# Wide scores and split value products for the last tile, three residuals by an identity product, and a new order table

## The chip, the cores and the metric

The kernel runs on one core of a Trainium2 chip. The metric is the device time of one execution in microseconds, median of the runs. The core's engines are TensorE (PE, with its weight loads PEld), VectorE (DVE), ScalarE (ACT), GpSimd (POOL) and SyncE (SP, which here only issues DMAs); each runs its own instruction stream in order, and semaphores tie them together.

## What is computed

Four attention layers over x of 2048 tokens by 512 features, each with a layer norm ahead and a residual behind. Layers 1 and 3 (A) are linear attention, layers 2 and 4 (B) are causal attention in a window of 256 keys; both have 32 heads of 16 features. The two A layers share weights, and so do the two B layers.

```python
def _A_ref(x, wqkv, wo):                       # linear attention, H = 32, Dh = 16
    q, k, v = ...                              # (x @ wqkv), split in heads
    phi = lambda t: jnp.where(t > 0, t + 1, jnp.exp(t)) + 1e-6
    pq, pk = phi(q), phi(k)
    kv = jnp.einsum("bhsd,bhse->bhde", pk, v)
    z = jnp.einsum("bhsd->bhd", pk)
    num = jnp.einsum("bhqd,bhde->bhqe", pq, kv)
    den = jnp.einsum("bhqd,bhd->bhq", pq, z)[..., None] + 1e-6
    o = num / den
    return o.transpose(...).reshape(B, S, D) @ wo

def _B_ref(x, wqkv, wo):                       # window W = 256
    q, k, v = ...
    scores = jnp.einsum("bhqd,bhkd->bhqk", q, k) * (Dh ** -0.5)
    mask = (idx[:, None] - idx[None, :] >= 0) & (idx[:, None] - idx[None, :] < W)
    p = _softmax(jnp.where(mask[None, None], scores, -1e9), axis=-1)
    o = jnp.einsum("bhqk,bhkd->bhqd", p, v)
    return o.transpose(...).reshape(B, S, D) @ wo

x = x + _A_ref(_layernorm(x), A_wqkv, A_wo)
x = x + _B_ref(_layernorm(x), B_wqkv, B_wo)
x = x + _A_ref(_layernorm(x), A_wqkv, A_wo)
x = x + _B_ref(_layernorm(x), B_wqkv, B_wo)
```

## The kernel before

The tokens are cut into 16 tiles of 128. Python code builds a list of some 2,500 operations (`Plan`), each with the engines that it may run on, what it reads and writes, and the PSUM tiles that it holds; one operation emits between one and 64 instructions. The order of the whole list, the engine of each operation that has a choice (ACT or DVE for PSUM evictions, DVE or POOL for some masks) and the PSUM bank of each tile stand in a packed literal, `TABLE`. `place` (L92) unpacks it; `synchronise` (L133) then works out which semaphores each operation has to wait for, and `play` (L1072) writes every engine's stream in the table's order. So an engine's order is that of the table, and a wait of one operation holds back all that stand behind it on its engine. The table was written by a search of its own, and only its result stands in the kernel.

PSUM has eight banks of 128 x 512 f32; nearly all work passes through them, with TensorE writing and ACT or DVE reading.

The stages, by time in the profile: layer 1's keys, queries and sums over all tiles (to about 44 us), layer 1's closing sums (`barrier`, L530), then layer 2 tile by tile, together with layer 3's keys and values of tiles that are done (`middle(2)`, L884); layer 3's closing sums (about 242 us); layer 4 tile by tile (`middle(3)`), and the output.

The steps that the change and the prediction touch:

- `setup` (L288): 12 loads on SP. x comes in pieces (tiles 0, 1, 2-3, 4-5, 6-7, 8-11, 12-15), the A weights as keys (`wAk`), queries (`wAq`), values (`wAv`) and output (`wAo`), the B weights as `wBn` (1 MB), `wBv` and `wBo`. An eighth and later load waits for the landing of the one four places ahead of it in this list.
- `norm` (L366): statistics on DVE (L374, L375), epsilon added to the variance (L377 on DVE for tile 0 alone, L379 on POOL for all others), the power -1/2 on POOL (L380), normalisation on DVE (L381), then a transpose, by DMA from SP or, for the first and last tiles of a stage, by TensorE with an eviction (L395, L402).
- `tok` (L410): a product of one tile with 512 columns, four matmuls in two halves; `resid` (L602) adds its PSUM result to the tile of x on DVE (L604).
- `b_scores` (L659): scores of a tile's 64 keys (b = 0 or 1, one half of the tile's 128 keys, each key twice for an even and an odd head) against up to 256 queries, for two of the four head groups f at once: 8 matmuls into four banks, two exps on ACT (L686), one causal mask on DVE (L694). A tile has four such groups.
- `b_first` (L702): for tile 0, half b = 0, the same over all four f, 128 queries at a time: 16 matmuls, two exps of 1024 columns (L721), a mask over 16 head groups (L726).
- `b_far`, `b_edge`, `far_masks`: scores and masks at the far edge of the window (L754, L772, L773, L801).
- `b_values` (L807): value products of a tile, one PSUM tile for each half h of the head groups; for each f and each of four heads pairs, up to six matmuls of 34 columns, one per block of 64 keys (L822), 24 instructions for one f; then reciprocal and division (L834, L835).
- `b_out` (L840): transpose, output product, residual. `b_last` (L849): the same for tile 15 of layer 4, in halves, with two residuals of 256 columns (L877) and two stores of 64 KB (L878). The other 15 tiles are stored by `outp` (L942) from SP or POOL.
- at the end SP waits for every DMA's semaphore in turn (L1103 to L1106).

## Time and profile before

| | |
|---|---|
| time, median of 3 runs (lowest, highest) | 412.12 us (411.43, 413.20) |
| the profiled execution | 412.60 us |
| its span, first to last instruction | 410.8 us |
| instructions | 17,540 |
| granted TensorE clock, mean | 1.000 |
| bytes moved by DMA | 37.19 MB |

The page gives for each engine the time in which it was busy and the share of the span. The chain that ended last is followed back from the last instruction, at each step to what released it; its shares say what set the end, by engine. A stage table gives the busy time of each engine within a stretch of the span, as "busy (x instructions)" in the order PE, PEld, DVE, ACT, POOL, then the granted clock, the DMA share and GB/s. A timeline row is start, length, engine, line, operation, output and input, shapes, count, and in brackets the idle time before it with what ended it. In a row of a group, the figures after the bar are busy time in us and the mean of one instruction in ns. A row of DMA issues ends with KB each and the median time from issue to landing.

### The profile page before, as it was taken

Reading aid. Unit: us, or ns where it says so; the run is one execution under the profiler, and the core shown is the slowest. Engines: PE = TensorE matmul, PEld = TensorE weight load, DVE = VectorE, ACT = ScalarE, POOL = GpSimd, SP = SyncE. Lnnn points to the kernel's source line nnn. Section 1 sums busy time; section 2 is a strip of 40 time slices with the busy share of each in tenths; the row PEclk is TensorE's granted clock in tenths of the full one; section 3 lists DMA queues with packets and bytes.
Section 4 is the critical chain, followed back from the end, with each engine's and each line's share of the span. In section 5 each row is a group of like instructions: output and inputs, shape, how many; then the busy total and the mean of one; then the engine's idle time right before and its main releaser. Section 6 shows DMA issues by size and latency. Waiting matters only on the chain.

```text
span 410.8 us, 17540 instructions
## 1 busy us (share of the span) xinstructions
PE 386.9 (94%) x7668; PEld 260.3 (63%) x7742; DVE 344.5 (84%) x807; ACT 352.8 (86%) x448; POOL 122.4 (30%) x216
## 2 busy tenths in 40 slices
PE   7999999999999999999999999999999988999896
PEld 3654676766575576566567777586757755566674
DVE  6997799989998899888887789997899688857585
ACT  4654659998999999999998357999999999999993
POOL 4576653111252331320503203303113304303020
PEclk9999999999999999999999999999999999999999
DMA  7495114443243435353222100344314821561751
GB/s 249 101 217 144 49 34 115 120 70 90 56 106 74 119 77 107 81 119 82 68 41 57 27 2 2 105 109 81 102 44 122 122 66 41 120 127 56 168 107 42
DMA packets 66596, 37.19 MB, mean 91 GB/s; under 512 B 47640, under 2 KB 61848, under 8 KB 66520
## 3 DMA queue, kind: packets, MB, share of 16 engines
q1 hardware_dynamic: 66032, 34.75, 37.0%
q8 instruction: 61, 1.00, 1.1%
q0 software_dynamic: 480, 1.31, 1.0%
q14 instruction: 15, 0.12, 0.1%
q10 hardware_dynamic: 8, 0.00, 0.0%
HBM read 6.29 MB, written 2.10 MB: 20 GB/s over the span
## 4 chain that ended last, share of the span: by engine, by line
PE 51%; ACT 34%; DVE 9%; DMA 3%; issue 2%; SPq 1%; POOL 1%
ACT pb L686 20%; PE ps L420 18%; PE ps L434 10%; PE ps L822 10%; PE ps L676 5%; ACT pb L801 5%; ACT vp L686 4%; PE ps L501 3%; ACT tE L444 2%; DMA wA<-in_A_wqkv_dram 2%; DMA xT<-xn 1%; DVE xres L604 1%; DVE stats L374 1%; ACT pb L721 1%; PE ps L477 1%
## 5 line engine op out<-in xcount | busy, mean ns | idle before, releaser
L686 ACT ACTIVATE pb<-ps 128x1024 bf16<-128x1024 f32 (+2 forms) x216 | 198.9, 1020 | 5.2 <-PE ps L676 3.9
L822 PEld LDWEIGHTS ps<-vB,pb 128*128 128x128 bf16 x2560 | 77.7, 96 | 12.3 <-DVE pb L694 3.6
L822 PE MATMUL ps<-vB,pb 128*128 128x34 bf16 x2560 | 83.5, 177 | 0.6 <-POOL pb L772 0.3
L434 PE MATMUL ps<-xT,wBp 128*128 128x128 bf16 x1024 | 69.0, 219 | 1.7 <-ACT tE L444 0.6
L434 PEld LDWEIGHTS ps<-xT,wBp 128*128 128x128 bf16 x1024 | 58.5, 98 | 13.7 <-issue 4.4
L379 POOL TENSOR_SCALAR ve<-mv 128x1 f32<-128x1 f32 x63 | 16.7, 265 | 154.7 <-DVE mv L375 152.7
L444 ACT ACTIVATE tE<-ps 128x512 bf16<-128x512 f32 x64 | 38.6, 612 | 27.1 <-PE ps L420 11.2
L772 POOL TENSOR_SCALAR_AFFINE_SELECT pb<-pb 128x1024 bf16<-128x1024 bf16 x30 | 34.4, 1146 | 71.4 <-DVE pb L694 23.8
L676 PE MATMUL ps<-XQ,kB 32*128 32x256 bf16 (+3 forms) x992 | 48.0, 267 | 3.3 <-ACT pb L754 0.7
L604 DVE TENSOR_TENSOR xres<-ps,xres 128x512 bf16<-128x512 f32 x63 | 43.0, 684 | 6.7 <-PE ps L420 6.3
L420 PE MATMUL ps<-wA,XQ 128*128 128x512 bf16 x174 | 45.6, 379 | 2.2 <-issue 0.6
L374 DVE BATCH_NORM_STATS2 stats<-xres 128x6 f32<-128x512 bf16 x64 | 43.5, 685 | 2.8 <-DMA xres<-in_A_x_dram 2.2
L694 DVE TENSOR_TENSOR pb<-pb,tri 128x512 bf16<-128x512 bf16 (+1 forms) x108 | 41.5, 396 | 3.3 <-ACT pb L686 3.1
L801 ACT ACTIVATE pb<-ps 128x1024 bf16<-128x1024 f32 x42 | 41.4, 1059 | 1.1 <-PE ps L792 0.9
L380 POOL TENSOR_TENSOR rs<-ve,negh 128x1 f32<-128x1 f32 x64 | 37.8, 591 | 8.3 <-DVE ve L377 3.0
L434 PE MATMUL ps<-XQ,wA 128*128 128x128 bf16 x512 | 35.4, 219 | 0.3 <-DMA wA<-in_A_wqkv_dram 0.3
L434 PEld LDWEIGHTS ps<-XQ,wA 128*128 128x128 bf16 x512 | 30.7, 98 | 7.3 <-DMA wA<-in_A_wqkv_dram 0.8
L420 PE MATMUL ps<-wBv,xT 128*128 128x512 bf16 x110 | 31.4, 380 | 2.6 <-issue 1.0
L676 PEld LDWEIGHTS ps<-XQ,kB 32*128 32x128 bf16 x992 | 15.0, 92 | 29.5 <-ACT pb L686 7.5
L420 PE MATMUL ps<-M,XQ 128*128 128x512 bf16 x113 | 30.7, 380 | 2.3 <-ACT vp L686 0.4
L420 PE MATMUL ps<-wBo,oT 128*128 128x512 bf16 x105 | 28.8, 380 | 2.8 <-issue 1.0
L686 ACT ACTIVATE vp<-ps 128x1024 bf16<-128x1024 f32 (+2 forms) x32 | 26.7, 928 | 1.5 <-PE ps L676 1.5
(126 smaller groups left out, 551.6 us busy)
## 6 DMA issues: line engine op xcount, KB each, us to landing
vB<-vS SPq DMA_DIRECT2D x64, 136.0 KB, 2.7
kB<-vp SPq DMA_DIRECT2D x60, 128.0 KB, 2.3
wA<-in_A_wqkv_dram SPq DMA_DIRECT2D x3, 512.0 KB, 5.5
out_dram<-xres POOLq DMA_DIRECT2D x10, 128.0 KB, 2.8
xres<-in_A_x_dram SPq DMA_DIRECT2D x2, 512.0 KB, 5.1
pb<-in_B_wqkv_dram SPq DMA_DIRECT2D x1, 1024.0 KB, 5.8
xres<-in_A_x_dram SPq DMA_DIRECT2D x3, 256.0 KB, 5.5
out_dram<-xres SPq DMA_DIRECT2D x5, 128.0 KB, 2.7
```

Source lines behind the costliest of these rows:

```text
L374: self.on("DVE", "stats", lambda e: e.bn_stats(K.stats[:, t, :], x()), key, dve(512), rd=rd, wr=[("stats", t)], **held)
L380: self.pow = self.on("POOL", "pow", lambda e: e.tensor_tensor(K.rs[:, t, :], K.ve[:, t, :], K.negh[:], ALU.pow), key + 0.03, (640, 690), r ...
L420: m = e.matmul(K.ps(ps), lhs(c), rhs(c), start=c == 0 and not whole, stop=c == 3)
L434: m = e.matmul(K.ps(ps)[:, f * P:(f + 1) * P], w(c, f), xT(c), start=c == 0, stop=c == 3)
L444: self.on("ACT", "E", lambda e: e.activation(K.tE[:, s, :], K.ps(ps), ACT.Exp, bias=0.0), key, act(512), wr=[("tE", s)], ps=[ps])
L604: self.on("DVE", "res", lambda e: e.tensor_tensor(K.xres[:, t, :], K.ps(po), K.xres[:, t, :], ALU.add), key, dve(512), rd=[("xres", t)], w ...
L676: m = e.matmul(K.ps(ps[gq])[:, ns * i:ns * i + ns], K.kB[rows, j % 4, 2 * f + b, :, :], K.XQ[rows, f, q:q + ns], start=True, stop=True, ti ...
L686: return e.activation(out(2 * h, 2, ns), i, ACT.Exp, bias=0.0, scale=0.25)
L694: return e.tensor_tensor(x, x, K.tri[:, 0, sh:64].unsqueeze(1).unsqueeze(1).to_broadcast([P, 4, n, 64 - sh]), ALU.mult)
L772: return e.affine_select(out=x, in_=x, compare_op=ALU.is_ge, fill=0.0, base=-2, pattern=[[0, 16], [-2, 64]], channel_multiplier=1)
L801: return e.activation(far(h), i, ACT.Exp, bias=0.0, scale=0.25)
L822: m = e.matmul(K.ps(ps)[:, 34 * u:34 * u + 34], K.P((b // 2) % rp)[:, gq, f, o:o + P], K.vB[:, (b // 2) % 4, b % 2, r, :], start=i == 0, s ...
```

## The change

It has five parts.

1. Tile 15's scores, in both B layers, are made over all four head groups at once: `b_first` becomes `b_wide`, which takes the tile, the half b, the queries and their width. For each b one burst of 16 matmuls, two exps (1024 columns for b = 0, 512 for b = 1) and one mask, in place of two groups of 8 matmuls, two exps and one mask each.
2. Tile 15's value products of layer 4 are in two parts: `pu` for the four blocks of earlier tiles' keys (16 matmuls for one f), `pv` for the tile's own two blocks (8 matmuls). Both add into one PSUM tile; only the very first matmul of a bank clears it.
3. Three residuals of layer 4 are added by TensorE, as a product of the identity with the tile of x, behind the output product: tiles 13 and 14 whole, and the second half of tile 15. The result is then copied by ACT or DVE in place of the addition on DVE. The first half of tile 15 is still added on DVE.
4. Tile 15's output leaves in one store of 128 KB in place of two of 64 KB.
5. The epsilon addition may run on DVE or POOL for every tile, and the table is new: order, engines and banks.

```diff
-WHOLE = {2: (), 3: ()}
+WHOLE = {2: (), 3: (13, 14)}
+SPLIT = {3: (15,)}
...
-            self.on("POOL", "eps", lambda e: e.tensor_scalar(K.ve[:, t, :], K.mv[:, t, 1:2], LN_EPS, None, op0=ALU.add), key + 0.02, (300, 330), rd=[("mv", t)], wr=[("ve", t)])
+            self.g.add("eps", {"POOL": (300, 330), "DVE": (66, 150)}, lambda e, eng: e.tensor_scalar(K.ve[:, t, :], K.mv[:, t, 1:2], LN_EPS, None, op0=ALU.add), key + 0.02, rd=[("mv", t)], wr=[("ve", t)])
...
-        if whole:
-            self.pe("id", lambda e: e.matmul(K.ps(ps), K.ident[:], K.xres[:, t, :], start=True, stop=False), key - 0.01, 1, 512, rd=[("xres", t), ("ident",)], ps=[ps])
...
+                if whole and h:
+                    m = e.matmul(K.ps(ps), K.ident[:], K.xres[:, t, :], start=False, stop=True)
...
+    def resid(self, t, po, key, whole=False):
+        K = self
         if whole:
+            self.copy("rs", po, lambda: K.xres[:, t, :], lambda: K.ps(po), key, 512, wr=[("xres", t)])
+            return
...
-    def b_first(self, p, key):
+    def b_wide(self, j, b, q, w, n, key):
...
+        sl = j % self.rp
+        c = 384 * b + q - P * j - 64 * b
...
-                    m = e.matmul(K.ps(ps[gq])[:, P * f:P * f + P], K.kB[rows, 0, 2 * f, :, :], K.XQ[rows, f, P * p:P * p + P], start=True, stop=True, tile_position=(32 * gq, 0))
+                    m = e.matmul(K.ps(ps[gq])[:, w * f:w * f + w], K.kB[rows, j % 4, 2 * f + b, :, :], K.XQ[rows, f, q:q + w], start=True, stop=True, tile_position=(32 * gq, 0))
...
+        if split:
+            before = [x for x in blocks if x[1] > 0]
+            blocks = [x for x in blocks if x[1] <= 0]
+            for f in (2 * h, 2 * h + 1):
+                def put(e, f=f):
+                    m = None
+                    for gq in range(4):
+                        u = 4 * (f - 2 * h) + gq
+                        for i, (b, c) in enumerate(before):
+                            m = e.matmul(K.ps(ps)[:, 34 * u:34 * u + 34], at(b, c, gq, f), val(b, 4 * f + gq), start=i == 0 and u == 0, stop=False, skip_group_check=True)
+                    return m
+                self.pe("pu", put, key - 0.002 - 0.001 * (f % 2), 16, 34, rd=reads(f, before), ps=[ps])
...
+                    if not h:
+                        m = e.matmul(K.ps(po)[:, 256:512], K.ident[:], K.xres[:, j, 256:512], start=False, stop=False, skip_group_check=True)
...
-        for n in range(2):
-            cs = slice(256 * n, 256 * n + 256)
-            self.on("DVE", "res", lambda e, cs=cs: e.tensor_tensor(K.xres[:, j, cs], K.ps(po)[:, cs], K.xres[:, j, cs], ALU.add), key + 0.2 + 0.1 * n, dve(256), rd=[("xres", j)], wr=[("xres", j, n)], ps=[po])
-            self.on("SP", "out", lambda e, cs=cs: e.dma_start(K.out[0, j * P:(j + 1) * P, cs], K.xres[:, j, cs]), key + 0.3 + 0.1 * n, (520, 2400), rd=[("xres", j, n)])
+        self.on("DVE", "res", lambda e: e.tensor_tensor(K.xres[:, j, 0:256], K.ps(po)[:, 0:256], K.xres[:, j, 0:256], ALU.add), key + 0.2, dve(256), rd=[("xres", j)], wr=[("xres", j, 0)], ps=[po])
+        self.copy("rs", po, lambda: K.xres[:, j, 256:512], lambda: K.ps(po)[:, 256:512], key + 0.3, 256, rd=[("xres", j)], wr=[("xres", j, 1)])
+        self.on("SP", "out", lambda e: e.dma_start(K.out[0, j * P:(j + 1) * P, :], K.xres[:, j, :]), key + 0.4, (520, 2400), rd=[("xres", j, 0), ("xres", j, 1)])
...
-                    if j + b == 0 and ph in PART:
+                    if j + b == 0:
                         if f < 2:
-                            self.b_first(f, base + 0.25 * f)
+                            self.b_wide(j, b, P * f, P, f, base + 0.25 * f)
+                    elif j == T - 1:
+                        if f == 0:
+                            self.b_wide(j, b, P * j + 64 * b, P - 64 * b, 0, base + j + b / 4)
...
 TABLE = (
-    r"c-qZZ1GH_+j;*AUO4YS(+qP}nwr$(CZQHhO+h*^z&%Lkz@5lf8{~o>0SxP0TnVDHN_6n(#3ZYPu0>vt{(khG!tBeY#;;UdPxccG}D67J&gzBTqtRkpSE~5J8",
...
+    r"c-pmB1K4IqvhJ#`s_q`!wr$(CZQHhO+qP}nwwcT%GfC#2^Zk?EB%9q#_TGEG|KP7Ky!BRfJ?Df{N`+Nn6spjQ6)8~Rl~#$Bs3gj%2r8+Hs0OI#E|O}aUb~m>",
...
```

What the two tables say, unpacked by the rule of `place` and named by the operations of the code: 2,559 operations before, 2,546 after. Of the operations in both, about three quarters on PE and seven eighths on ACT stand in the same order as before, and somewhat more than half on DVE. These change their engine: 21 epsilon additions from POOL to DVE; 13 far masks from POOL to DVE and 13 the other way; 17 evictions from ACT to DVE and 13 from DVE to ACT (sums and products that are copied counted in); ten stores between SP and POOL, which leaves eight on POOL instead of ten.

The orders at the two ends of the program (a number is a tile; k, q and g are halves of layer 1's key, query and sum products, T transposes; s scores with key half b and head groups, ex exps):

```
SP first    before  x0 x1 x2-3 wAk x4-5 wAq x6-7 x12-15 x8-11 T5 T6 T7 wBn T9 T8 wAo ... wAv wBv wBo
            after   x0 x1 x4-5 x2-3 wAk wAq x6-7 wAv x8-11 x12-15 T5 wBn T6 T7 T11 T8 T9 ... wAo T13 wBo
DVE first   before  stats0 aggr0 eps0 stats1 aggr1 norm0 stats2 aggr2 norm1 stats3 aggr3 norm2 stats4 stats5
            after   stats0 stats1 aggr1 aggr0 eps0 stats4 stats3 norm0 aggr3 aggr4 norm1 eps4 stats2 aggr2 stats5 norm4
PE first    before  fill2x T0 fill3x T1 k0 k0 fill T2 k1 k1 q1 T3 q1 q2 k2 k2 T4
            after   fill5x T0 T1 fill k0 k0 k1 k1 T3 q0 q0 T2 T4 q1 q1 q3 q3
PE last     before  pv14f0 s15b1f01 pv14f1 s15b0f01 pv14f2 s15b0f23 pv14f3 bout13 s15b1f23 pv15f0 T14
                    pv15f1 pv15f2 pv15f3 T15a bout14 T15b bout15 (3 parts)
            after   pv14f0 pv14f1 s15b1 pu15f0 pu15f1 s15b0 pv14f2 pv14f3 bout13+id pu15f2 T14 pv15f0
                    pv15f1 pu15f3 pv15f2 pv15f3 bout14 T15a bout14+id T15b bout15+id (3 parts)
ACT last    before  ex14 (last of it) ex15b1f01 x2 ex15b0f01 x2 ex15b0f23 x2 ex15b1f23 x2 evict T14 T15a T15b
            after   ex14 (last of it) ex15b1 x2 ex15b0 x2 copy13 evict T14 T15a copy15 (second half)
DVE last    after   ... mask15b0 rcp15 div15 rcp15 div15 evict T15b copy14 add15 (first half)
```

175 lines of the change are left out of this document (89 added, 86 removed).

## The prediction

> **What bounds the kernel now.** I read the page's busy shares and its chain first, then the busy time of each engine stage by stage, then the two places that the diff touches most: the first 12 us and the last 15 us.
>
> ```profile
> span 410.8 us, 17540 instructions
> ...
> PE 386.9 (94%) x7668; PEld 260.3 (63%) x7742; DVE 344.5 (84%) x807; ACT 352.8 (86%) x448; POOL 122.4 (30%) x216
> ...
> PE 51%; ACT 34%; DVE 9%; DMA 3%; issue 2%; SPq 1%; POOL 1%
> ```
>
> The shares are an average over stages with different limits, so I cut the span at the orders' own marks: from the first layer-1 product that waits for its weights to the end of layer 1, from the first to the last full exp group of layer 2, and the same for layer 4. Columns: PE, PEld, DVE, ACT, POOL busy; the last row here is DVE alone.
>
> ```profile
> 9.80:43.80 34.00, 33.26 (x283) 18.80 (x288) 29.26 (x80) 17.84 (x31) 22.14 (x47) 1.00 0.62 157
> 62.90:207.00 144.10, 137.51 (x2831) 91.47 (x2858) 128.86 (x297) 140.43 (x162) 40.09 (x67) 1.00 0.41 91
> 259.00:398.60 139.60, 130.58 (x3107) 90.04 (x3128) 111.80 (x258) 137.75 (x159) 32.45 (x49) 1.00 0.44 95
> ...
> 44.50:127.00 82.50, 77.83 (x178) 1.00 0.33 76
> ```
>
> Layer 1 is TensorE's (33.26 of 34.00 us): a microsecond lost at its start is not made good. The two long stretches are ScalarE's (140.43 of 144.10 and 137.75 of 139.60): what leaves ACT there is worth about its own time, if DVE keeps up, and DVE is 94% busy from 44.5 to 127.
>
> **The change, term by term.** The sum goes against the profiled execution's 412.60 us (span 410.8 and 1.8 around it); the median of the runs, 412.12, lies 0.48 below, which I take off at the end. Unpacked, the new table differs from the old in four ways that can cost or gain, and the code gives a fifth.
>
> **1. The start.** The loads leave SP in another order: x of tiles 4-5 now goes ahead of tiles 2-3 and of the key weights (wA). DVE's order follows: the statistics of tiles 4 and 3 stand ahead of tile 0's normalisation.
>
> ```profile
> xres<-in_A_x_dram SPq DMA_DIRECT2D x1, 256.0 KB, 3.7
> wA<-in_A_wqkv_dram SPq DMA_DIRECT2D x1, 512.0 KB, 4.6
> xres<-in_A_x_dram SPq DMA_DIRECT2D x1, 256.0 KB, 5.5
> ```
>
> ```profile
> 1.71 0.51 SPq L294
> ...
> 2.27 0.47 SPq L297
> ...
> 2.78 0.51 SPq L294
> ...
> 3.33 6.42 DMA wA<-in_A_wqkv_dram
> ```
>
> The first fence has the third, fourth and fifth load with their time to landing, the second when each was issued (the last row is the query weights, issue to landing). Landings: 1.71+3.7 = 5.4, 2.27+4.6 = 6.9, 2.78+5.5 = 8.3, 3.33+6.42 = 9.75. Each ends 1.4 us or so after the one issued before it, so they share a pipe in issue order. Key weights that leave fifth land at about 8.3 instead of 6.9; tiles 4-5 at 5.4, tiles 2-3 between 6.2 and 6.8.
>
> ```profile
> 4.81 0.38 DVE L381 TENSOR_SCALAR vp<-xres,mv,rs 128x512 bf16<-128x512 bf16 x1
> 5.42 0.69 DVE L374 BATCH_NORM_STATS2 stats<-xres 128x6 f32<-128x512 bf16 x1 [0.23 <-DMA xres<-in_A_x_dram]
> 5.93 0.60 ACT L402 ACTIVATE XQ<-ps 128x512 bf16<-128x512 bf16 x1 [2.63 <-PE ps L395]
> 7.15 1.03 PE L420 MATMUL ps<-wA,XQ 128*128 128x512 bf16 x4
> 9.79 0.62 PE L434 MATMUL ps<-XQ,wA 128*128 128x128 bf16 x8 [0.32 <-DMA wA<-in_A_wqkv_dram]
> ```
>
> Now: tile 0 is normalised at 4.81 and its transposed copy is out at 5.93+0.60 = 6.53, so 1.72 us later; the key products start at 7.15, just behind their weights. After: the statistics of tile 3 end 0.6 to 0.7 us past the landing at 6.2 to 6.8, tile 0's normalisation starts at 6.9 to 7.5, its copy is out at 8.6 to 9.2, and the first four half products, two matmuls at 0.22 each (worked out under (c)), 1.72 in all, end at 10.3 to 10.9. With the same products behind it TensorE stood at 9.79. So the start costs 0.5 to 1.1 us, and as layer 1 is TensorE's, all of it stays. I take the upper end, +1.1, as the transposes of tiles 2 to 4 and a 1 MB load, now ahead of DMA transposes, stand in line too; bounds +0.4 and +1.8.
>
> **2. Layer 2's exp stretch.** Five evictions leave ACT there (two of queries, one each of keys, values and the next layer's values), three come (two of queries, one of keys).
>
> ```profile
> L407 ACT ACTIVATE XQ<-ps 128x512 bf16<-128x512 f32 x9 | 5.4, 605 | 0.6 <-PE ps L434 0.6
> L627 ACT ACTIVATE vp<-ps 128x512 bf16<-128x512 f32 x7 | 5.4, 777 | 0.7 <-PE ps L434 0.6
> L407 ACT ACTIVATE vS<-ps 128x512 bf16<-128x512 f32 x6 | 4.3, 712 | 0.0
> L375 DVE BATCH_NORM_AGGREGATE mv<-stats 128x2 f32<-128x6 f32 x64 | 11.0, 175 | 0.8
> ```
>
> Two queries and one of keys cancel; two evictions of some 0.6 to 0.7 remain, -1.3, or -1.1 as back-to-back operations overlap by a tenth. Against it DVE takes these, and nine of the 21 epsilon additions that move from POOL to DVE fall into 44.5 to 127; the nearest row, a DVE instruction on 2 columns, is 0.175, so 1.6 at most, some 1.1 with the overlap. I take -0.8: DVE had 82.50-77.83 = 4.7 us of gaps, which take the additions. Bounds -1.1 and, with DVE the limit throughout, +1.2.
>
> **3. Tile 15's scores of layer 2** become two bursts of 16 matmuls instead of four groups of 8.
>
> ```profile
> 258.53 0.40 PE L712 MATMUL ps<-XQ,kB 32*128 32x128 bf16 x16
> ...
> 399.21 0.29 PE L676 MATMUL ps<-XQ,kB 32*128 32x128 bf16 x8
> ```
>
> A burst of that width exists already: 0.40 against 2x0.29 for its two halves, and much of the 0.18 is the tail of a group, which the next one overlaps. Worth -0.1 (0 to -0.3) where TensorE sets the pace, as I take it to do between the two exp stretches.
>
> **4. Layer 4's exp stretch.** Between its first and last full exp, two key evictions and one of queries leave ACT, one of queries and one of values come: 2x0.777+0.605-0.605-0.712 = 0.84, with overlap -0.7. DVE is 80% busy (111.80 of 139.60) and covers them. Bounds -1.3 (the first score burst stands 1.5 us of products earlier in TensorE's order) and +0.6 (DVE late at the stretch's start, where it takes three key evictions).
>
> **5. The end.**
>
> ```profile
> 397.66 0.76 PE L822 MATMUL ps<-vB,pb 128*128 128x34 bf16 x24
> 398.64 0.66 ACT L686 ACTIVATE vp<-ps 128x256 bf16<-128x256 f32 x2
> 399.56 2.08 ACT L686 ACTIVATE vp<-ps 128x512 bf16<-128x512 f32 x4 [0.26 <-PE ps L676]
> 402.30 0.66 ACT L686 ACTIVATE vp<-ps 128x256 bf16<-128x256 f32 x2 [0.66 <-PE ps L676]
> 405.99 0.69 DVE L604 TENSOR_TENSOR xres<-ps,xres 128x512 bf16<-128x512 f32 x1 [0.27 <-PE ps L420]
> 407.19 0.88 DVE L877 TENSOR_TENSOR xres<-ps,xres 128x256 bf16<-128x256 f32 x2 [0.51 <-PE ps L871]
> 408.10 0.38 SPq L878 DMA_DIRECT2D out_dram<-xres  x1
> ```
>
> ```profile
> L721 ACT ACTIVATE pb<-ps 128x1024 bf16<-128x1024 f32 x8 | 7.7, 1030 | 0.5 <-PE ps L712 0.5
> L726 DVE TENSOR_TENSOR pb<-pb,tri 128x1024 bf16<-128x1024 bf16 x2 | 1.4, 676 | 0.0
> ...
> out_dram<-xres SPq DMA_DIRECT2D x1, 128.0 KB, 2.1
> out_dram<-xres SPq DMA_DIRECT2D x2, 64.0 KB, 1.6
> ...
> out_dram<-xres SPq DMA_DIRECT2D x5, 128.0 KB, 2.7
> ```
>
> Now the last tile's exps run from 398.64 to 402.96. In the new TensorE order both halves of tile 14's first value products, 24 matmuls or 0.6 us each, stand ahead of the first burst; now only one does. So ACT, whose full groups end as the row at 398.64 begins, waits until about 399.2. Then two exps of 512 columns (to 400.3) and, behind the second burst, which waits for two banks of the first and for two parts of value products, two of 1024: 400.5 to 402.5. The exps end 0.5 earlier. But the mask is now one instruction on all heads (0.68 instead of 0.42), and all of tile 15's own-block products, 32 matmuls, and one earlier-block part of 16 stand behind it at 0.025 each (the row at 397.66 less one matmul's 0.18, over 23): 1.2 us to 404.5, against 404.8 now. The identity product of tile 14 (0.2) then stands ahead of the last transpose, so that ends as now. From there the output halves are finished by DVE and ACT side by side, DVE behind tile 14's copy: both done at 407.6, not 408.07. One store of 128 KB follows instead of two of 64 KB: by the rows of the end 2.1 instead of 1.6, so +0.5. Sum -0.1. Of the three identity products the first and third lie under the exps and under the last eviction. Bounds -1.0 (bursts not starved) and +0.8 (the store at 2.7, as the page has the median for five from SP).
>
> On the store, the row says 0.5 us for 64 KB more. The Trainium skill, DMA: Bandwidth & Descriptors, section "Anatomy of one DMA", puts most of a transfer's time in a fixed 2.0 us and the rest at 436 GB/s; by that 64 KB would add 0.15, an estimate, and the end would be -0.45.
>
> Sum: +1.1 - 0.8 - 0.1 - 0.7 - 0.1 = -0.6, so 412.0 against the profiled execution and **411.5** against the median.
>
> **The rivals.** *(a) The gains come, the start is free.* If the third to fifth loads are held by issue and not by a shared pipe, the start costs nothing; with the other terms at their better bounds 412.1 - 1.1 - 0.2 - 1.3 - 0.9 = **408.6**. For it: ACT is 97 to 99% busy in both long stretches and loses work in each. Against it: four landings in a row, in issue order.
>
> *(b) DVE takes the place of ACT.* 21 epsilon additions and, on balance, more evictions go to an engine with gaps of 4.7 us in 82.5. It decides once the additions meet no gap between 44.5 and 127. Then 412.1 + 1.1 + 1.2 - 0.1 + 0.6 - 0.1 = **414.8**: slower. For it: the 94%. Against it: the shorter way from statistics to normalisation, which has one engine fewer in it.
>
> *(c) TensorE cools at the start.* Between its fill products and the delayed first product TensorE would idle about 2 us; its wait before the row at 9.79 was 0.32.
>
> ```profile
> PEclk9999999999999999999999999999999999999999
> ...
> 1.65 3.28 PE L1082 MATMUL ps<-kB 128*128 128x512 bf16 x8
> ...
> 405.14 0.81 PE ps L420 x3
> ```
>
> Eight cold matmuls take 3.28, three warm ones of that size 0.81: with the last one's 0.63 and 0.38 taken off, 0.38 against 0.22 from start to start. If 3.3 us ran cold again, 1.4 us more would be lost: 412.1 + 1.8 + 1.4 - 1.7 + 0.4 = **414.0**, the other terms a little short of mine. Against it: the page's clock row has nine tenths or more in every slice, the early waits included. The Trainium skill, TensorE: Matmul & The Clock Gate, Part 1, has the array fall back to half its clock after an idle window of some 3.4 us; a gap of 2 us would then mostly pass, and no run here shows where the limit is.
>
> That the bursts don't do what they say is in term 5: the first starves for 0.6 us.
>
> **How the numbers follow.** Forecast 0.42, (a) 0.28, (b) 0.18, (c) 0.12. A measurement of this kernel tells about 0.5% from no change, so 410.06 and 414.18 are the limits. Faster: most of (a), 0.27, and the forecast's edge, 0.05, make 0.32. Slower: 0.14 of (b), 0.05 of (c), 0.02 of the forecast, 0.21. The rest, 0.47, is within. The forecast's own range is 410.2 to 413.2. The whole range reaches to 408.4, just under (a), and to 415.0, just over (b); it leaves out some 0.1 on each side, the worse half of each.
>
> **What would show it.** Start: key weights landing at 8.3, the first key product past 8.5, the first query product at 10.4 to 11.2; a query product at 9.8 refutes term 1. Middle: first exp of layer 2 later by about the same, the exp stretches shorter by 0.8 and 0.7; DVE at 98% from 44.5 to 127 with ACT gaps beside it would be (b). End: an ACT gap of about 0.6 ahead of the first burst's exps, last exp to span's end 8.2 us (now 7.8). The forecast is wrong as a whole if the stretches change by more than 2 us, which would be orders that fit the chip better or worse than prefix sums can tell.

## The result and the profile after

The changed kernel takes **415.58 us** (median of four runs, 414.99 to 415.94) against 411.85 in the runs beside it: ratio 1.0071, interval 1.0048 to 1.0094. It is slower, by 3.7 us, where 411.5 was forecast. Its profiled execution took 415.94, 3.34 more than that of before.

The page of the changed kernel: span, busy time of each engine, the chain that ended last, and from the list of DMA queues the code that the sequencers fetch.

```profile
span 414.2 us, 17610 instructions
...
PE 396.9 (96%) x7745; PEld 261.5 (63%) x7745; DVE 346.2 (84%) x826; ACT 350.8 (85%) x438; POOL 116.5 (28%) x193
...
q8 instruction: 61, 1.00, 1.1%
...
PE 55%; ACT 25%; DVE 12%; DMA 5%; POOL 1%; issue 1%; SPq 0%; POOLq 0%; DVEq 0%
```

ScalarE's work fell by 2.0 us, as the moved copies promise, and the span grew all the same: in the chain ScalarE went from 34% to 25%, and TensorE, VectorE and transfers took its place. The same stages as before (columns PE, PEld, DVE, ACT, POOL; the last row is VectorE alone), cut at the same operations:

```profile
10.50:44.20 33.70, 33.32 (x297) 19.21 (x295) 29.60 (x83) 16.93 (x30) 22.66 (x45) 1.00 0.69 157
63.50:210.00 146.50, 141.86 (x2859) 91.57 (x2858) 132.08 (x313) 139.78 (x160) 33.56 (x51) 1.00 0.44 91
260.80:401.90 141.10, 134.58 (x3130) 90.86 (x3130) 112.45 (x259) 137.48 (x158) 33.94 (x44) 1.00 0.44 96
...
45.30:128.00 82.70, 78.10 (x186) 1.00 0.35 77
```

Both exp stretches hold less ScalarE work (139.78 for 140.43, 137.48 for 137.75) and are longer (146.50 for 144.10, 141.10 for 139.60). What grew is ScalarE's idle time in them: 6.7 instead of 3.7 us, and 3.6 instead of 1.9. VectorE is 94% busy from 45.3 to 128, just as before.

To see where it went I took the start of one and the same operation in both traces, after less before. The lag is +0.60 at layer 2's first exp (63.49 for 62.89), +2.89 at an exp that stood at 194.6, +2.32 at layer 4's first exps (261.7), +3.30 at its last full ones (397.7) and 3.4 at the end. So: start +0.6, layer 2's stretch +2.3, its end with barrier 2 -0.6, layer 4's stretch +1.0, the tail +0.1.

The largest single step, from +1.0 to +2.8, lies between the exps that stood at 138.7 and 149.2. Rows of the changed kernel's timeline there, one of each engine (in brackets the idle time ahead of the row and what ended it):

```profile
137.10 1.27 SPq L389 DMA_TRANSPOSE XQ<-xn  x1
...
141.23 0.41 DVE L381 TENSOR_SCALAR xn<-xres,mv,rs 128x512 bf16<-128x512 bf16 x1 [1.81 <-DMA XQ<-xn]
...
142.34 0.40 PE L582 MATMUL ps<-rec,spread 32*128 32x128 bf16 x16 [1.41 <-DVE vp L632]
...
142.33 0.66 ACT L407 ACTIVATE vS<-ps 128x512 bf16<-128x512 f32 x1 [0.53 <-issue]
143.75 0.60 ACT L447 ACTIVATE tE<-ps 128x512 bf16<-128x512 f32 x1 [0.76 <-PE ps L418]
```

Read it upwards: ScalarE waits for TensorE, TensorE for the key copy that VectorE makes (L632), and VectorE stands still because the normalisation of tile 5 writes the one buffer from which the transpose of tile 4, issued at 137.10, still reads. The new order has the normalisation of tile 4 (xn of t4) 3.4 us later than before, 1.0 of it the lag, behind the residual of tile 5.

### The profile page after: what moved, and what is told of

It reads as the page before. It is cut to its first block, busy times and chain, and to the rows that moved or that the text cites. A ratio compares the mean times of both kernels' runs of the same rounds, so it can differ in the third digit from the quotient of the medians.

```text
span 414.2 us, 17610 instructions
## 1 busy us (share of the span) xinstructions
PE 396.9 (96%) x7745; PEld 261.5 (63%) x7745; DVE 346.2 (84%) x826; ACT 350.8 (85%) x438; POOL 116.5 (28%) x193
## 3 DMA queue, kind: packets, MB, share of 16 engines
q0 software_dynamic: 384, 1.05, 0.8%
## 4 chain that ended last, share of the span: by engine, by line
PE 55%; ACT 25%; DVE 12%; DMA 5%; POOL 1%; issue 1%; SPq 0%; POOLq 0%; DVEq 0%
PE ps L418 19%; ACT pb L690 15%; PE ps L437 14%; PE ps L851 9%; PE ps L680 5%; ACT vp L690 4%; ACT pb L807 3%; DVE stats L374 2%; DVE vp L454 1%; DMA XQ<-vp 1%; DMA wA<-in_A_wqkv_dram 1%; PE ps L798 1%; DMA xT<-xn 1%; ACT tE L447 1%; DMA XQ<-xn 1%
## 5 line engine op out<-in xcount | busy, mean ns | idle before, releaser
L690 ACT ACTIVATE pb<-ps 128x1024 bf16<-128x1024 f32 (+1 forms) x208 | 195.5, 1044 | 5.7 <-PE ps L680 4.9
L851 PEld LDWEIGHTS ps<-vB,pb 128*128 128x128 bf16 x2496 | 75.0, 96 | 13.3 <-DVE pb L698 4.5
L851 PE MATMUL ps<-vB,pb 128*128 128x34 bf16 x2496 | 81.2, 177 | 1.1 <-ACT pb L690 0.3
L680 PE MATMUL ps<-XQ,kB 32*128 32x256 bf16 (+1 forms) x928 | 46.2, 272 | 4.8 <-ACT pb L690 1.3
L418 PE MATMUL ps<-wA,XQ 128*128 128x512 bf16 x192 | 49.2, 379 | 1.2 <-DMA wA<-in_A_wqkv_dram 0.6
L379 POOL TENSOR_SCALAR ve<-mv 128x1 f32<-128x1 f32 x42 | 11.0, 262 | 109.1 <-DVE mv L375 107.8
L418 PE MATMUL ps<-wBv,xT 128*128 128x512 bf16 x128 | 34.6, 380 | 0.0
L418 PE MATMUL ps<-M,XQ 128*128 128x512 bf16 x128 | 33.5, 380 | 0.7 <-ACT vp L690 0.4
L418 PE MATMUL ps<-wBo,oT 128*128 128x512 bf16 x124 | 33.3, 380 | 0.1
L418 PEld LDWEIGHTS ps<-wA,XQ 128*128 128x128 bf16 x192 | 16.4, 97 | 19.1 <-issue 1.6
```

The costliest lines, as they stand in the source:

```text
L418: m = e.matmul(K.ps(ps), lhs(c), rhs(c), start=c == 0, stop=c == 3 and not whole)
L680: m = e.matmul(K.ps(ps[gq])[:, ns * i:ns * i + ns], K.kB[rows, j % 4, 2 * f + b, :, :], K.XQ[rows, f, q:q + ns], start=True, stop=True, ti ...
L690: return e.activation(out(2 * h, 2, ns), i, ACT.Exp, bias=0.0, scale=0.25)
L851: m = e.matmul(K.ps(ps)[:, 34 * u:34 * u + 34], at(b, c, gq, f), val(b, 4 * f + gq), start=i == 0 and not split, stop=i == len(blocks) - 1 ...
```

## The experiments

The order was edited in the unpacked table; the diffs show the moved lines of it, an engine's name ahead of the operation. Each run was timed in five rounds against the kernel before on the same chip (before: 412.0 to 412.7). The four columns on the right are the steps of the lag in the run's own profile, taken as above: up to layer 2's first exp, over its stretch, over its end and barrier 2, over layer 4's stretch. They are of one execution each, and executions differ: e4 and f2 run the changed kernel's very order up to layer 4, and yet their start is up to 1.0 and their layer 2 up to 1.35 from its values. Nor do they add up to the medians beside them: the profiled execution of h5 took 419.17, that of h1 417.19, that of h4 415.52. A number behind the name of an operation in the diffs and expectations counts operations of its kind and isn't always the tile's: normalisation 12 is that of tile 4.

| run | us (ratio, interval) | start | layer 2 | barrier | layer 4 |
|---|---|---|---|---|---|
| the changed kernel | 415.58 (1.0071, 1.0048 to 1.0094) | +0.60 | +2.29 | -0.57 | +0.98 |
| e1 normalisation 12 earlier | 417.08 (1.0121, 1.0085 to 1.0156) | +0.43 | +3.00 | -0.45 | +1.00 |
| e2 epsilons and masks back | 417.43 (1.0118, 1.0095 to 1.0140) | +1.04 | +1.64 | +0.09 | +1.94 |
| e3 layer 1 as before | 416.48 (1.0093, 1.0071 to 1.0115) | +1.08 | +2.89 | -0.45 | +0.65 |
| e4 transpose 11 earlier | 415.30 (1.0064, 1.0040 to 1.0088) | +1.57 | +0.94 | -0.45 | +1.11 |
| f1 layers 1, 2 as before | 412.60 (1.0005, 0.9980 to 1.0031) | -0.36 | +0.05 | -0.51 | +1.12 |
| f2 layer 4 as before | 416.05 (1.0074, 1.0048 to 1.0099) | +1.14 | +1.19 | +0.80 | -0.15 |
| f3 both as before, new tail | 413.07 (1.0017, 0.9993 to 1.0041) | -0.39 | +0.03 | +0.84 | -0.61 |
| f4 copies' engines as before | 421.67 (1.0194, 1.0149 to 1.0238) | +1.92 | +4.66 | +0.82 | +1.73 |
| g1 code shifted a little | 414.90 (1.0066, 1.0042 to 1.0089) | +0.32 | +1.66 | -0.13 | +0.87 |
| g2 joined orders | 413.01 (1.0014, 1.0000 to 1.0027) | +0.00 | +0.23 | -0.51 | +1.79 |
| g3 copies alone on f1 | 413.71 (1.0042, 1.0027 to 1.0057) | -0.35 | +1.20 | -0.40 | +1.06 |
| g4 layer 2 as before | 414.39 (1.0045, 1.0027 to 1.0064) | +2.26 | +0.14 | -0.47 | +0.49 |
| h1 code shifted far | 416.27 (1.0088, 1.0068 to 1.0108) | +1.33 | +1.59 | -0.46 | +2.24 |
| h3 before, shifted far | 415.13 (1.0070, 1.0049 to 1.0092) | +0.16 | +0.62 | +0.12 | +0.72 |
| h4 four places mended | 417.21 (1.0123, 1.0095 to 1.0151) | +1.51 | +1.71 | -0.38 | +0.33 |
| h5 epsilons, masks alone on f1 | 417.45 (1.0119, 1.0083 to 1.0155) | +0.10 | +6.40 | +0.22 | +0.13 |
| k1 before, one block | 413.58 (1.0045, 1.0017 to 1.0074) | +0.82 | -0.31 | +0.01 | +0.65 |
| k2 before, half a block | 417.63 (1.0133, 1.0103 to 1.0164) | +1.07 | +4.21 | +0.01 | -0.15 |

**First round: the visible waits.** e1, the buffer wait at 141:

```diff
+DVE 2.xn t4
 DVE 2.E1 s0
...
+SP  2.T t4
 SP  2.vd t15
...
-DVE 2.xn t4
...
-SP  2.T t4
```

> The changed kernel with two operations moved in the order: layer 2's normalisation of tile 4 (xn of t4 on VectorE) goes back ahead of the E1 of slice 0, and its transpose goes back ahead of the value copy of tile 15 on SyncE. In the changed kernel VectorE stands still for 1.81 us at 141.23 because xn of t5 writes the buffer that the transpose of t4, issued only at 137.10, still reads. Theory 1 (that one wait made the step of 1.9 us between 138.7 and 164.7): the wait goes, the ScalarE gaps of 0.52 and 0.76 after it go, and the time falls by 1.5 to 1.9, to 413.7 to 414.1. Rival 2 (VectorE as a whole is overloaded by the 21 additions of epsilon and the 13 masks it was given): the wait moves on to another VectorE operation, less than 0.5 is gained. Rival 3 (the loads at the start set everything): nothing is gained, 415.6.

It gained nothing. The waits of e1's VectorE in the same stretch (us in total, times, longest):

```profile
DVE vp L632 <- PE ps L418: 2.0, 1, 2.0
DVE xres L608 <- PE ps L418: 0.2, 1, 0.2
```

The wait for the transpose is gone, and the next VectorE instruction, the key copy, stands 2.0 us in its place. The view puts that down to TensorE, but the product that it copies was done by 140.4. The copy also waits for a key transfer that reads the buffer it writes: issued at 138.09, that lands at 142.04, after 4.0 us, and the copy starts at 142.12. So it was not one operation's place; what set both free is the landing of a transfer. The view of DMA issues (median us from issue to landing) has them. First the key transfer and the transpose of tile 4 in the changed kernel, then the same transpose in e4, where this part of the order is the same and the lag grew by 0.5 only:

```profile
kB<-vp SPq DMA_DIRECT2D x1, 128.0 KB, 4.1
XQ<-xn SPq DMA_TRANSPOSE x1, 4.0
```

```profile
XQ<-xn SPq DMA_TRANSPOSE x1, 2.5
```

In one run the transfer takes 4.0, in the other 2.5. The packets of the trace show what stood ahead: in the changed kernel a block of code, one packet of 16 KB, is on its way from 133.49 to 135.07 and another from 138.49 to 139.70. Packets of 4 and 256 bytes of data that begin at 134.1 take 1.7 to 1.9 us each, those that begin near 139.0 up to 1.5, and in e1 the key transfer of 138.09 has a block beside it from 139.10 to 140.68. The row of rates from the issue of the transpose on (137 to 141 us in 40 slices, GB/s):

```profile
GB/s 227 287 369 369 123 21 20 184 410 410 266 41 0 31 307 195 215 202 200 179 57 3 0 0 0 0 3 8 8 10 8 10 10 10 18 3 0 76 98 120
...
q8 instruction: 1, 0.02, 1.9%
```

A packet counts where it starts: from 139.1 to 140.7 hardly one does. Till the block ends there is next to none, then some 10 GB/s, until the packets that began near 139.0 end together at 140.5, and the landing waits for them. The Trainium skill, DMA: Bandwidth & Descriptors, section "Queues, rings and completion order", has each engine turn to another queue only between whole packets; the waits here, 1.7 to 1.9 us beside a block of 1.58 and up to 1.5 beside one of 1.21, agree with it.

e2 asked for VectorE's load; it sets back the engine of 47 operations and moves none.

```diff
-DVE eps (21), mf (13)   POOL mf (13)
+POOL eps (21), mf (13)  DVE mf (13)
```

> The changed kernel with all additions of epsilon and all far masks on the engines that they had before (21 epsilons back from VectorE to GpSimd, 13 masks back from VectorE to GpSimd, 13 from GpSimd to VectorE), everything in the changed order. Theory 1 (places in the order, not VectorE's load): the 1.81 us wait at 141.2 stays; only the place at 91 us, where two masks stand on VectorE ahead of value product 8, can gain, so 414.7 to 415.9. Rival 2 (VectorE's load is what costs): 412.1 to 413.5, the whole loss or most of it. Rival 3 (start): 415.6.

417.43: taking the work off VectorE does not bring the time back. e3 (order, engines and banks of before up to 48.8 us) and e4 (`3.T t11` ahead of `3.oT 5` on SyncE) asked for the start and for one place in layer 4.

> The changed kernel with the order, the engines and the PSUM banks of the kernel before for the first 48.8 us (the loads, layer 1 and barrier 1 up to layer 2's first linear-attention product), and the changed order from there on. Theory 1: the start is worth what the lag is at the first exps of layer 2, 63.49 against 62.89, so 0.6 is gained at most, 415.0, and the wait at 141 stays. Rival 2 (VectorE's load): 415.3 to 415.6. Rival 3 (the later key weights set the pace up to the end): 1.1 or more is gained, 414.5 or below, and the later stretches shorten too.

> The changed kernel with one transfer moved: layer 4's transpose of tile 11 (T.11) ahead of the output transpose 5 (oT.5) on SyncE, as before. In the changed kernel SyncE waits 3.52 us for the output of oT.5 with T.11 behind it, its landing is late, and TensorE waits 0.94 for it at 331.6 ahead of query product 22; ScalarE then waits 0.93 at 333.06. Theory 1 (places in the order): 0.3 to 0.5 is gained (the lag steps from +2.5 to +2.9 there), 415.1 to 415.3. Rival 2 (VectorE's load: normalisation 11 itself comes late, at 322.87): 0 to 0.1, 415.5. Rival 3: 415.6.

e3 gained nothing: its lag at the first exps is +1.08 all the same, behind the join, and the stall at 139 is there again. In e4 the mended place did what was expected of it (the lag falls from +2.37 to +1.79 over it, where it rises from +2.57 to +2.94 in the changed kernel), but between the exps that stood at 353 and 379 it rises from +1.94 to +3.50. ScalarE and TensorE there (waits, us in total, times, longest):

```profile
PE ps L418 <- DVE pb L698: 0.9, 1, 0.9
...
ACT vp L690 <- PE ps L680: 1.1, 1, 1.1
```

The 0.6 gained is spent, and more, where TensorE stands 0.9 for a mask of VectorE's and the exps 1.1 behind it.

**Second round: the order by stages.** f1 to f3 join the two orders at places where few tiles are alive.

```diff
 f1: before's order to 216 us | changed
 f2: changed to 260 us | before's to 398 us | changed tail
 f3: before's to 216 us | changed to 260 us | before's to 398 us | changed tail
```

> Order, engines and PSUM banks of the kernel before up to layer 2's first scores of tile 15 (216 us); the changed order from there on: the end of layer 2, barrier 2, layer 4 and the new tail. Theory 1 (the loss sits in the order's places: 0.6 at the start, 2.3 in layer 2's exp stretch, 0.9 in layer 4, the barrier wins 0.4): 412.1 - 0.4 + 0.9 + 0.1, so 412.5 to 413.2. Theory 2 (chance of a 16 KB code block standing ahead of a transfer on one DMA engine, with any order alike): 413 to 416. Theory 3 (the new tail's code costs, the order doesn't): 415 to 416.

> The changed order up to the start of layer 4's exps (260 us), then order, engines and banks of the kernel before for layer 4 up to its first scores of tile 15 (398 us), then the new tail. Theory 1: layer 4's 0.9 comes back and the first layers' 2.5 stays: 414.3 to 415.0. Theory 2: 413 to 416. Theory 3: 415 to 416.

> Order, engines and banks of the kernel before everywhere but for the end of layer 2 with barrier 2 (216 to 260 us) and the tail (from 398 us), which are the changed kernel's: its bursts, halves of the value product, identity products and single store. Theory 1: 412.1 - 0.4 + 0.1, so 411.5 to 412.3. Theory 2: 412 to 415. Theory 3 (the tail's code costs): 414.5 to 416.

f1 is back at the time of before, f2 keeps the whole loss, f3 shows that the new code of the tail costs no more than the interval tells. (f2 and f3 came out 1.1 and 0.8 above what theory 1 gave them, f3 in the range of theory 2.) So, with the nine warming matmuls that all these runs have, the loss belongs to the changed order of layers 1 and 2. Layer 4's changed order costs 0.5 to 1.1 in the six profiles that have it as it is and the old warming (the changed kernel, e1, e3, f1, g3, g4), the barrier wins 0.4 to 0.6 in them, and f1 has both. f2 and f3 have the new barrier too, but lose 1.2 at their join, among layer 4's first exps.

f4 keeps the changed order and puts 30 copies and kindred steps back on the engines of before.

> The changed kernel with the 30 copies out of PSUM and kindred steps that changed engines (17 from ScalarE to VectorE, 13 the other way) back on the engines of before, in the changed order. It asks whether ScalarE's work paces the exp stretches: with that (the prediction's terms 2 and 4) the time grows by what ScalarE gets back, about 0.9 in layer 2 and 0.9 in layer 4, to 417.0 to 417.5. If the scores' arrival paces them instead (ScalarE's idle time in the stretches grew by 6 us while its work fell by 3), the time stays within 0.6 of 415.6.

Six us more, over three times the 1.8 that ScalarE got back: neither reading. It doesn't show that ScalarE's work has such a weight, for runs that leave ScalarE's work alone moved as far (e2 by 1.9 against the changed kernel, h5 below by 4.9 against f1).

**Third round: what in layer 2, and the code blocks.** g3 puts only the eight copies of layer 2's exp stretch that change engines on the new engines, in the old order: term 2 of the prediction by itself.

```diff
 f1 with, in layer 2:
-ACT bqe 5, bve 4, bqe 11, bke 10, ve 2    DVE bqe 4, bke 5, bqe 12
+DVE bqe 5, bve 4, bqe 11, bke 10, ve 2    ACT bqe 4, bke 5, bqe 12
```

> The run with layers 1 and 2 in the order of before, and in layer 2's exp stretch the eight copies out of PSUM that change engines put on the changed kernel's engines (ScalarE gives five to VectorE and takes three from it); the order stays. Term 2 of the prediction taken alone (ScalarE's work paces the stretch): the exps at 216 us come 0.8 earlier than in that run, 411.8. The other theory (a copy off ScalarE is worth nothing by itself, because the scores of the next exps are not there earlier, or VectorE gives them late): the lag there changes by less than 0.3, or grows; 412.6 or more.

The exps at 194.6 come 1.2 later than f1's, not 0.8 earlier, and 1.1 of it arises between 138 and 168 us. The busy times of that stretch in f1 and in g3 (columns PE, PEld, DVE, ACT, POOL), then g3's waits there (us in total, times, longest):

```profile
138.00:168.00 30.00, 29.77 (x608) 19.43 (x606) 26.94 (x64) 29.14 (x35) 8.53 (x14) 1.00 0.47 92
```

```profile
138.00:168.00 30.00, 29.01 (x589) 18.81 (x588) 26.99 (x63) 27.69 (x32) 8.52 (x14) 1.00 0.40 94
```

```profile
ACT pb L690 <- PE ps L680: 1.8, 3, 0.9
...
PE ps L851 <- DVE xres L608: 0.2, 1, 0.2
PE ps L680 <- DVE o L857: 0.2, 1, 0.2
PE ps L680 <- ACT XQ L407: 0.2, 1, 0.2
```

In f1 TensorE is as full as ScalarE here (29.77 of 30.00 us) and has no wait on the list; ScalarE waits 0.7 for scores. In g3 TensorE waits three times: for a residual and a division that VectorE now finishes later, and for a query copy that ScalarE took over. The scores come later by that, and ScalarE waits 1.8 for them. No transfer is among these waits.

h5, the same test for epsilons and masks (27 engine changes on f1):

> The run with layers 1 and 2 in the order of before (412.6), with the epsilon additions and far masks of both layers on the changed kernel's engines (17 epsilons to VectorE, six masks to VectorE, four masks to GpSimd), the order as before. Theory 1 (VectorE has room for them in this order): 412.3 to 413.0. Theory 2 (VectorE's own load is what the changed order suffers from): 413.5 to 415, as the eight copies alone cost 1.1.

417.45 (419.17 in the profiled execution), +6.4 in layer 2. Its VectorE from 138 to 168 us (waits as above):

```profile
DVE vp L632 <- DMA kB<-vp: 2.4, 1, 2.4
DVE tE L450 <- ACT tE L447: 1.3, 2, 0.7
```

Here VectorE does not lack time, it stands behind a transfer. The two largest steps, 3.3 us at 141 and 1.6 at 153 (f1's times), each have a late one: a key transfer issued at 137.26 lands after 3.9 us, beside a code block from 137.98 to 139.58, and a transpose issued at 152.42 after 4.7, beside one from 154.57 to 156.04. g4 and g2 join further.

> The changed order up to layer 2's first scores (63 us), the order of before from there to 216 us, the changed order for the rest. With the run that had layer 1 alone as before (416.5) it parts the start from layer 2. Theory 1 (start 0.6, layer 2's stretch 2.3): 0.6 above the run with both as before, 413.0 to 413.5. The other (the later start is what costs, by where it puts every transfer later): 414.5 to 416.

> The order of before to 216 us, the changed order for the end of layer 2, barrier 2 and layer 4 up to the score burst 16 (293 us), the order of before from there to 398 us, the new tail. Theory 1 (places in the order): the changed order's barrier wins 0.5 (lag -0.31 to -0.82 in the run with layers 1 and 2 as before), the later part of layer 4 in before's order does not lose the 1.1 that the changed order lost there: 411.0 to 412.0. If the pieces do not add up: 412.5 to 413.5.

g4's layer 2 loses nothing (+0.14); its join costs 1.66 of idle ScalarE ahead of the first exps, so it doesn't size the start. g2 doesn't add up the best pieces: layer 4 loses 1.8 in it. No run beats the kernel before.

The phase runs leave the order alone and change how many instructions TensorE runs ahead of it, so that its code blocks fall elsewhere:

```diff
-for _ in range(9): matmul of 512 columns
+g1: 5 of them and 28 of 32 columns    h1, h3: 1 and 113
+k1: 137 of 32 columns                 k2: 73
```

> The changed kernel with the nine warming matmuls ahead of everything exchanged for five of them and 28 short ones of 32 columns: TensorE runs 24 more matmuls (48 instructions with their weight loads), so every 16 KB block of its code is fetched about 0.9 us earlier (59 such blocks lie about 5 us apart in the trace); nothing else is changed. Theory A (in layer 2 at 133 to 141 us pieces of SyncE's transfers stand 1.5 to 1.9 us behind a code block on one DMA engine, and that is 1.3 of the 1.8 us that are lost there): the packets over 1 us are at other places, the step of the lag between the exps at 138.7 and 149.2 us is 0.5 instead of 1.8, and the time is 414 to 414.5 if no other transfer on the path is hit. Theory B (the order alone loses it): the step stays at 1.8 and the time at 415.6.

> The changed kernel with the nine warming matmuls exchanged for one of them and 113 short ones of 32 columns: 105 more matmuls, 210 instructions of 256 to a code block, so a block's start stands about 46 instructions (some 0.9 us) later in the work than in the changed kernel, as it stood by chance in the runs without the stall. Theory A (a code block ahead of SyncE's pieces at 133.5 to 136 makes 1.4 of the 1.8 us lost between the exps at 138.7 and 149.2 us): the step there is 0.3 to 0.6, and the time 414.2 (with no new hit on the path). Theory B (order alone): step 1.4 to 2.0, 415.6.

> The kernel before with the same exchange of warming matmuls: what the place of the code blocks does without any change of the order. If the order before has slack for its transfers, no more than 0.5 either way: 411.7 to 412.7. If its 412.1 is itself a lucky place of the blocks: 413.5 or more.

g1 moved the blocks by less than meant (one starts at 132.72), packets stand behind it again at 133.6, and the step between the two exps is 1.41: it tells nothing apart. In h1 no data packet from 132 to 142 us takes over 0.8 us and the step is 0.48, as theory A said (e4 and f2 have 0.47 and 0.46 there with the old warming, by chance); but the total is 416.27, since layer 4 now loses 2.2. And h3 shows that the kernel before has no such slack either: 415.13 with not one operation moved.

h1 and h3 together are a second comparison of the two kernels, with the same exchange on both sides and timed beside each other. There the change costs 1.1 us, not 3.7, and the two intervals (1.0068 to 1.0108, 1.0049 to 1.0092) overlap. Their profiles differ by +1.17 at the start, +0.97 in layer 2, -0.58 at the barrier and +1.52 in layer 4; they are a slow execution of h1 (417.19) and the fastest of h3 (414.36), so only the signs should be read from them.

> The changed kernel with the far exchange of warming matmuls and with four operations put earlier: layer 2's scores 15 ahead of value product 8 on TensorE, normalisation 12 and its transpose as in the first experiment, layer 4's transpose 11 ahead of output transpose 5. Theory 1 (single places): 1.4 from the stall, 0.4 at 93 us, 0.4 in layer 4: 413.2 to 413.8. Theory 2 (each wait removed comes back as the next one, since the order's transfers all run at their limit): 414.5 to 415.6.

All places mended and the stall avoided (its step is 0.46): 417.21, above both ranges. One wait came back as another: my own move of scores 15 made the gap ahead of its exps 1.79 instead of 1.05.

The last two runs part the place of the blocks from the exchange of warming matmuls.

> The kernel before with its nine warming matmuls exchanged for 137 short ones: 128 more, 256 instructions, one whole 16 KB block, so the blocks' bounds stand at the same places of the work as in the kernel before. Theory A (the place of the code blocks against the transfers made the exchange of the run before cost 0.7%): 411.9 to 412.9. Theory B (the exchange itself costs, by a TensorE that is warmed otherwise or a later start): 414.5 to 415.5.

> The same with 73 short ones: 64 more matmuls, 128 instructions, half a block. Theory A: other transfers are hit, so another time than 412.4, by 0.5 to 3 us, and packets over 1 us at other places than in the kernel before. Theory B: the same as with a whole block.

k1, where the blocks stand as in the kernel before, takes 413.58, k2 417.63; both lie above theory A's ranges. The exchange itself costs something (k1's interval lies above 1), but the 4.05 between the two, same order and same kind of exchange, goes with the place of the code blocks. The start differs by 0.25 only, layer 2 by 4.5. Three transposes of layer 2 make most of that: they land after 2.5, 2.4 and 2.4 us in k1 and after 4.1, 3.7 and 4.1 in k2, where a code block stands beside each. TensorE waits 0.7, 0.9 and 1.2 for them, and ScalarE 3.5 in these three places, for 0.3 in k1's. The third is issued at 172 us in k1 and at 176 in k2. k1:

```profile
xT<-xn SPq DMA_TRANSPOSE x1, 2.4
```

k2, the piece of its chain and the TensorE row behind it:

```profile
175.59 4.10 DMA xT<-xn
```

```profile
179.83 1.05 PE L434 MATMUL ps<-xT,wBp 128*128 128x128 bf16 x16 [1.22 <-DMA xT<-xn]
```

In the kernel before it took 2.4 as well. In k2 a code block goes from 177.65 to 178.58, and the landing comes 1.7 us later than in k1.

## Why the prediction was wrong

**The step that failed is term 2**, and with it term 4: "what leaves ACT there is worth about its own time, if DVE keeps up". Term 2 said -0.8; the copies alone, without the rest of the order, cost 1.2 (g3), and the whole changed order of that stretch cost 0.9 to 2.3 in the five profiles that share it (the changed kernel, e4, f2, g1, h1). Term 4 said -0.7 and measured +1.0 (+0.5 to +1.1 over six profiles). The prediction gave the two long stretches to ScalarE alone (140.43 of 144.10 us), but its own row has TensorE at 137.51 of the same 144.10, and the chain had 51% TensorE and 34% ScalarE. Where TensorE is full too, work that leaves ScalarE only makes it wait for scores; g3 shows that with 29.77 of 30.00 us. The condition was read from busy shares as well: VectorE kept up in work, but not in time. An engine that runs its list in order passes every wait of its own on: in g3 VectorE's residual and division came late and held TensorE up. ScalarE did lose the work; it got it back as idle time.

The second thing that the sum lacked is a term for the landing of a transfer and for a buffer that is still being read. In the profile of the changed kernel, 1.8 of layer 2's 2.3 us arise at one such place (139 us), in e4 and f2 with the same order 0.5, and their layer 2 cost 0.9 and 1.2, as much as the copies alone in g3. So the order by itself costs about 1, and the rest came with transfers that were late in that execution; this split is an estimate from these profiles.

**Term 1 held.** Key weights were to land at 8.3, the first key product to stand past 8.5, the first query product at 10.4 to 11.2. The chain and the timeline of the changed kernel:

```profile
2.80 5.67 DMA wA<-in_A_wqkv_dram
```

```profile
8.61 1.89 PE L418 MATMUL ps<-wA,XQ 128*128 128x512 bf16 x8 [0.64 <-DMA wA<-in_A_wqkv_dram]
...
10.56 1.06 PE L437 MATMUL ps<-XQ,wA 128*128 128x128 bf16 x16
```

Landed at 8.47, then 8.61 and 10.56. At layer 2's first exp +0.60 of the +1.1 was left in this profile; four profiles with this start and the old warming (the changed kernel, e1, e4, f2) have 0.43 to 1.57, mean 0.94, and six with the old one (the kernel before, f1, f3, g2, g3, h5) -0.39 to +0.10, mean -0.17. The means differ by 1.1, as forecast, though the four alone are spread over as much; h1 and h3 differ by 1.17. e3, which has the old start and +1.08 behind its join, isn't counted.

**Term 3** (-0.1) lies in the step over layer 2's end and the barrier, -0.6; its share was not taken apart.

**Term 5**: ScalarE was to wait 0.6 ahead of the bursts' exps, and 8.2 to lie from the last exp to the end.

```profile
402.91 3.16 ACT L727 ACTIVATE vp<-ps 128x512 bf16<-128x512 f32 x4 [0.79 <-PE ps L718]
...
411.12 0.38 ACT L407 ACTIVATE xres<-ps 128x256 bf16<-128x256 f32 x1 [1.83 <-DVE xres L900]
...
411.53 0.33 SPq L902 DMA_DIRECT2D out_dram<-xres  x1
```

It waited 0.79, and from 406.07 to 414.2 are 8.1. The wait came as forecast; the exps won 0.2 instead of 0.5. That the end took 8.1 is luck, for two parts of it were wrong. The output halves were not finished side by side: ScalarE's copy at 411.12 waits 1.83 for VectorE's addition at L900, because `Graph.add` lets each user of a PSUM tile wait for the one before it, and both read the same tile. From the last exp to the last half it took 5.4 us, where 5.1 had been counted. And the single store cost less:

```profile
out_dram<-xres SPq DMA_DIRECT2D x1, 128.0 KB, 1.7
```

That is 0.1 more than the 1.6 of 64 KB, not 0.5. The row with 2.1 that the term took was a store issued at 404.04, beside a code block from 403.69 to 405.00; the 0.15 that the prediction took from the Trainium skill, DMA: Bandwidth & Descriptors, section "Anatomy of one DMA", was near, though that section times GpSimd's path and this store is SyncE's. The sum is +0.1 instead of -0.1.

**The rivals.** (b) gave 414.8, the nearest number, by the wrong mechanism: its mark, VectorE at 98% from 44.5 to 127, is not there (78.10 of 82.70), and taking the additions off VectorE did not help (e2). (c) is out by the row at 8.61: eight matmuls of 512 columns in 1.89, which is 0.22 from start to start, the warm value. The granted clock can't tell, for it is 1.00 from 1.60 to 4.95 of the kernel before too, where such matmuls took 0.38. (a) is out by term 1. The last sentence of the prediction named the true case, orders that fit the chip worse "than prefix sums can tell", and gave it no price or chance; the range ended at 415.0.

What stays open: how much of the 3.7 us belongs to the changed order and how much to where its transfers happen to fall against the code blocks. One order alone takes from 412.1 (the kernel before) to 417.6 (k2) by the exchanges that move the blocks, the changed one 414.9 to 416.3 in the three places tried (the changed kernel, g1, h1). Of the transposes past 45 us whose landing the trace has, 29 of 72 took over 3.3 us in the changed kernel, 17 of 68 before, 20 of 72 in k1, 26 of 72 in k2, but 19 of 71 in h1, which is slow too; so their number alone does not make the time, and which of them lie on the path was shown for single cases only.

## What to carry to other kernels

A fixed order fits its engines and its transfers as one thing. Before a copy taken off one engine is counted as a gain, look whether a second engine is as full in that stretch (here TensorE beside ScalarE); and price the copy by what waits behind it on its new engine and by the buffer that it frees or holds, not by its own duration. Where a transfer's landing has two values (here 2.5 and 4.1), look whether the order still works with the larger. And before two orders are compared within 1%, shift the code of both by half a block once and see how far each moves by itself.

## What was not expected of the hardware

The fetch of code delays data. The changed kernel's trace has 61 blocks of 16 KB, one for some 256 instructions of TensorE, each on its way for 0.9 to 1.7 us and mostly 4 to 9 us apart. All of its 29 transposes that took over 3.3 us to land had such a block on the way within 2.6 us of their issue, and 14 of the other 43 (in the kernel before 17 of 17, and 19 of 51). The late ones land mostly after 3.3 to 4.5 us, the others after 2.2 to 2.8. Between k1 and k2, shifting the blocks of one order by half a block moved the time by 4 us, 1%, more than the whole change did. The Trainium skill, Runtime: NRT & Kernel Launch, section "Instruction fetch mechanics", calls the cost of such a block "mostly hidden". No run here measures what it costs the engine that fetches; k1 and k2 show a cost at the transfers beside it.
